# Attention in turns of two slots, with the second sigmoid written to SBUF

## The chip, the cores and the metric

The kernel runs on one core of a Trainium2 chip. A core has TensorE (PE) for matmuls, VectorE (DVE), ScalarE (ACT) and GpSimd (POOL) for elementwise work, and SyncE (SP), from whose queue most transfers are issued. The metric is the device time of one execution in microseconds (us). Before the change it was 1052.52 us, the median of three runs (1050.96 to 1053.29).

## The reference

Three stages follow each other: a sigmoid attention, a mixture of experts with one expert per token, and a feed-forward layer. The change is in the attention alone:

```python
def _attn_ref(q, k, v):                      # each (4, 12, 448, 64)
    S = q.shape[2]
    scale = 1.0 / np.sqrt(q.shape[-1])
    scores = scale * np.matmul(q, k.transpose(0, 1, 3, 2)) - np.log(S)
    attn = 1.0 / (1.0 + np.exp(-scores))
    return np.matmul(attn, v).astype(np.float32)
...
    x = attn_out.transpose(0, 2, 1, 3).reshape(B * S, H * D)   # 1792 tokens x 768
    x = _moe_ref(x=x, **moe_kwargs)          # 8 experts, argmax routing, relu, gate weight
    return _moe2_ref(x=x, **moe2_kwargs)     # (h - tanh(h)) @ w_out
```

## The kernel before, in words

All matmul operands are split into a high part (rounded to the matmul's format) and a low part (the rest), and each product is three matmuls: high by high, low by high, high by low.

The 12 heads of the 4 batches are 24 pairs of two heads. `load` brings the raw keys and queries of a pair into a buffer `kq` (three of them, in turn) and its values into `vr`; all go out from SP's queue. `prep` makes the high part `w..h` from `kq` on DVE (L199) and the low part `w..l` on POOL (L202, two operations); `prep_v` makes `vh` on DVE (L210) and `vl` on POOL (L211), two operations each.

The scores are computed transposed, 128 keys by 448 queries. Two heads of a pair have three full tiles of 128 keys each and a rest of 64 keys; two pairs together are seven **slots**: three of the first pair, one shared slot with both pairs' rests, three of the second pair. Each slot holds two tiles of 128 x 448. In six of the seven slots the two tiles of a step are two matmuls over 64 rows of the array, which run side by side; in the shared slot they are matmuls over all 128 rows, one after the other. There are 84 slots.

For a slot `u`, `scores(u)` issues the score matmuls into `pq` in PSUM (L233; three buffers of two banks in the pool `ps2`, which `pr` of `rows` and `prank` of the routing also use). ACT then computes the sigmoid twice from `pq`: once rounded, into `ah` in SBUF (L240), and once in full, back into `pq` in PSUM (L241). DVE subtracts the two into `al` (L242). Three slots later (`LAG` = 3) `av` sums attention by values: six matmuls over 128 rows into `pav` (L256). When the last slot of a pair is summed, `pav` is copied to `xT`; `rows` transposes it on PE into `pr` (L281), which DVE copies out as `u` and `rec`. When a batch's last pair is through, its tokens are routed: `square` on ACT (L298), and `route_a`, `gate` and `route_b` with many small DVE operations.

The order on PE in the attention is the written one (`manual_schedule`): for each slot the scores, then the sums of three slots before, then what `plan` put at that slot (`prep`, `load`, `rows`, routing). The other engines' order is set by a scheduler from the program's order and its own estimates. A buffer comes free when its last reader is done.

Of the kernel before, what the change touches and what calls it, by code (L numbers as in the profile page):

```python
# [10 lines left out]
F32 = mybir.dt.float32  # L11
F32R = mybir.dt.float32r
BF16 = mybir.dt.bfloat16
I32 = mybir.dt.int32
U32 = mybir.dt.uint32
AF = mybir.ActivationFunctionType
ALU = mybir.AluOpType
# [4 lines left out]
LAG = 3  # L22
# [3 lines left out]
CONV = 14  # L26
# [3 lines left out]
P = 128  # L30
CP = 112
# [3 lines left out]
def f32(ap):  # L35
    return ap.bitcast(F32)


class Prog:
# [90 lines left out]
    def attention(self):  # L130
# [4 lines left out]
        nc, tc = self.nc, self.tc  # L135
# [10 lines left out]
        pav2 = self.pool("aps3", 2, cx, space=PSUM)  # L146

        self.ep = pers
        NV, NW, NK = 2, 2, 3
        KW = 4 * P  # L150
        kqs, ws, vhs, vls = [], [], [], []

# [19 lines left out]
        def load(i):  # L172

            b, j = pairs[i]
            kq = kqs[i % NK]
            k, q = self.k[b, j], self.q[b, j]
            for dst, src in (
                (kq[:D, KW:], q[:, :S]),
                (kq[D:, KW:], q[:, S:]),
                (kq[:D, :S], k[:, :S]),  # L180
                (kq[D:, : 3 * P], k[:, S + HK :]),
                (kq[D:, S:KW], k[:, S : S + HK]),
            ):
                nc.sync.dma_start(dst, src)
            vr = raw.tile([P, 2, 4, D], F32, tag="vr", name="vr")
            self.w_dma = nc.sync.dma_start(vr.rearrange("p h c d -> p (h c d)"), self.v[b, j])
            st[i] = dict(kq=kq, vr=vr)

        def prep(i):

            s = st[i]
            kq, (h, l) = s["kq"], ws[i % NW]
            s["w"] = (h, l)
            ks, qs = slice(0, KW), slice(KW, KW + S)
            if i == 0:
                nc.vector.tensor_copy(h[:, qs], kq[:, qs])
                nc.scalar.copy(h[:, ks], kq[:, ks])
            else:
                nc.vector.tensor_copy(h, kq)  # L199
            for x in (qs, ks):  # L200
                eng = nc.vector if i == 0 else nc.gpsimd
                eng.tensor_tensor(l[:, x], kq[:, x], f32(h[:, x]), ALU.subtract)  # L202
# [21 lines left out]
        def scores(u):  # L224
            hi = sp.tile([P, 2, S], F32R, tag="ah", name="ah", bufs=LAG + 2)
            lo = sp.tile([P, 2, S], F32R, tag="al", name="al", bufs=LAG + 2)
            tiles[u] = (hi, lo)
            pq = ps2.tile([P, 2, 512], F32, tag="qk", name="pq")
            for m, (kt, qt) in enumerate(((0, 0), (0, 1), (1, 0))):
                for x, (i, a, c, _) in enumerate(slots[u]):  # L230
                    w = st[i]["w"]
                    p = slice(0, P) if a == 2 else slice(a * D, (a + 1) * D)
                    nc.tensor.matmul(  # L233
                        pq[:, x, :S], w[kt][p, c : c + P], w[qt][p, KW:], start=(m == 0), stop=(m == 2)
                    )
            k = len(slots[u])
            pv = pq[:, :k, :S]
            sc = dict(bias=self.bias_s, scale=1.0 / math.sqrt(D))
            hi, lo = hi[:, :k], lo[:, :k]
            nc.scalar.activation(hi, pv, AF.Sigmoid, **sc)  # L240
            self.last_sig = nc.scalar.activation(pv, pv, AF.Sigmoid, **sc)  # L241
            nc.vector.tensor_tensor(lo, pv, f32(hi), ALU.subtract)  # L242

        def av(u):
            hi, lo = tiles.pop(u)
            for x, (i, a, c, o) in enumerate(slots[u]):
                s = st[i]
                vh, vl = s["v"]
                if "pav" not in s:
                    s["pav"], s["units"] = pav2.tile([P, 512], F32, tag="av", name="pav"), 0  # L250
                pav = s["pav"]
                vo = lambda t: t[:, o : o + 2].rearrange("p h d -> p (h d)")
                b0, e = s["units"] == 0, s["units"] == 6
                s["units"] += 1
                for m, (vv, aa) in enumerate(((vh, hi), (vl, hi), (vh, lo))):
                    nc.tensor.matmul(  # L256
                        pav[:, :S], vo(vv), aa[:, x], start=(b0 and m == 0), stop=(e and m == 2)
                    )
                if e:
                    b, j = pairs[i]  # L260
                    if j == 0:
                        self.bts[b] = dict(
                            rec=self.recs[b % 2],
                            ss=self.sm.tile([CP, NCH], F32, tag="ss", name="ss"),
                            u=xp.tile([CP, NCH, E], F32, tag="u", name="u"),
                        )
                    s["xT"] = xp.tile([P, S], F32, tag="xT", name="xT")
                    if i % 2:
                        nc.scalar.copy(s["xT"], pav[:, :S])
                    else:  # L270
                        nc.vector.tensor_copy(s["xT"], pav[:, :S])  # L271
# [22 lines left out]
                nc.gpsimd.tensor_copy(rec[:, :, self.DM : self.DM + 1], self.tok[:, b].unsqueeze(2))  # L294

        def square(bt, c):
            sq = xp.tile([CP, NJ * P], F32, tag="sq", name="sq", bufs=1)
            nc.scalar.activation(sq, bt["rec"][:, c, : NJ * P], AF.Square, accum_out=bt["ss"][:, c : c + 1])  # L298

        self.cv, self.n_early = None, NEARLY  # L300
# [1 line left out]
        def conv():  # L302

            while self.units and self.n_early:
                if self.cv is None:
                    self.cv = self.conv_steps(*self.units[0], after=self.w_dma)
                    self.units.pop(0)
                with tc.high_priority(offset=LATER):
                    r = next(self.cv, 1)
                if r is None:  # L310
                    return
                self.cv = None
                self.n_early -= 1
# [13 lines left out]
            warm = self.cp.tile([P, 1], F32, name="warm")  # L327
            nc.scalar.activation(warm, self.bias_s, AF.Sigmoid)
        prep(0)
        for i in (1, 2):  # L330
            if i < n:
                load(i)
        if n > 1:
            prep(1)
        prep_v(0)
        pe = {mybir.EngineType.PE}
        with tc.manual_schedule(engines=pe):
            at = {}

            def plan(u, f, *args):  # L340
                at.setdefault(u, []).append((f, args))

            def events(u):
                while at.get(u):
                    f, args = at[u].pop(0)
                    f(*args)
                at.pop(u, None)

            def route(i):
                b = pairs[i][0]  # L350
                bt = self.bts.pop(b)
                for c in range(NCH):
                    plan(now[0] + 1 + c // 2 if b < B - 1 else now[0], square, bt, c)
                r = self.route_a(bt)
                pr = lambda: ps1.tile([P, 2, 512], F32, tag="qk", name="prank")
                if b == B - 2:
                    plan(now[0] + ROUTE_E - 1, self.gate, b, r)
                    plan(now[0] + ROUTE_E, self.route_b, b, r, pr)
                    plan(now[0] + ROUTE_E, self.send_rows, b, r)
                    plan(now[0] + ROUTE_E, self.early_rows)  # L360
                    plan(ns, self.early_gates)
                    plan(ns + 1, self.early_columns, lambda: ps2.tile([P, 2, 512], F32, tag="qk", name="xt"))
                elif b < B - 1:
                    plan(now[0] + ROUTE - 1, self.gate, b, r)
                    plan(now[0] + ROUTE, self.route_b, b, r, pr)
                    plan(now[0] + ROUTE, self.send_rows, b, r)
                else:
                    self.last_route = b, r

            for i in range(n):  # L370
                if i >= 2:
                    plan(final[i - 2] + 1, prep, i)
                if i >= 3:
                    plan(final[i - 3] + 2, load, i)
                if i >= 1:
                    plan(first[i] + LAG - 2, prep_v, i)
                plan(final[i] + LAG + ROW + (3 if i == 0 else 0), rows, i)
                if pairs[i][1] == NJ - 1:
                    plan(final[i] + LAG + ROW, route, i)
            plan(5, self.embedding)  # L380
            now = [0]
            u = 0
            while u < ns + LAG:
                now[0] = u
                if u < ns:
                    scores(u)
                if LAG <= u < ns + LAG:
                    av(u - LAG)
                events(u)
                if u >= CONV:  # L390
                    conv()
                if u == ns and self.cv is not None:
                    for _ in self.cv:
                        pass
                u += 1
        while at:
            now[0] = u
            events(u)
# [772 lines left out]
```

## Time and profile before

| what | value |
|---|---|
| median of three runs | 1052.52 us |
| the profiled execution | 1052.65 us |
| its span | 1050.9 us |
| PE, DVE, ACT, POOL busy | 97%, 79%, 53%, 16% of the span |
| mean granted TensorE clock | 0.995 |
| the last `pr` of the attention starts on PE at | 238.08 us |

The profile gives, for one execution, the busy time of each engine, and the trace lists every instruction with its start, its duration and, where the engine was idle before it, what released it. Matmuls are pipelined, so that a PE row lasts longer than the step to the next row; the steps between starts tell the pace.

### The profile page before, as it was taken

To read this page: it belongs to the slowest core of one execution; us is meant where nothing else is said; L and a number is where in the kernel's file an instruction comes from. 1 tells how busy PE (TensorE), PEld (TensorE's weight loads), DVE (VectorE), ACT (ScalarE), POOL (GpSimd) and SP (SyncE) were. 2 spreads that over 40 slices of the span, in tenths; PEclk is the share of its full clock that TensorE was granted. 3 is DMA by queue.
4 is the path that set the end of the run, shared out by engine and by line. 5 is a ranking of instruction groups with operands and counts; after the bars stand their busy time and mean duration, and the time that the engine had idled before them with its cause. 6 is when DMAs were issued, how large, how long until landed. Compare 5 with 4: busy or idle time off the path is not lost.

```text
span 1050.9 us, 16813 instructions
## 1 busy us (share of the span) xinstructions
PE 1016.5 (97%) x6437; PEld 939.6 (89%) x6437; DVE 828.9 (79%) x1172; ACT 557.0 (53%) x694; POOL 166.4 (16%) x178
## 2 busy tenths in 40 slices
PE   7999999899999999999998999999999999999997
PEld 5777777678999999999997899999999999999997
DVE  7879797978968878889963798888987676766774
ACT  6778787777666666666643544442453322332230
POOL 7345546342021001010000000000000300000002
PEclk9999999999999999999999999999999999999999
DMA  5422424338878984874922535454443522332212
GB/s 160 140 83 82 134 65 142 118 115 299 297 243 299 337 290 162 282 257 161 309 103 94 197 139 175 180 210 150 181 151 120 193 94 89 120 120 98 113 61 106
DMA packets 83527, 175.28 MB, mean 167 GB/s; under 512 B 7639, under 2 KB 62958, under 8 KB 83438
## 3 DMA queue, kind: packets, MB, share of 16 engines
q1 hardware_dynamic: 79598, 155.78, 43.2%
q0 software_dynamic: 3840, 18.35, 4.9%
q8 instruction: 52, 0.85, 0.3%
q14 instruction: 37, 0.30, 0.1%
HBM read 156.68 MB, written 36.30 MB: 184 GB/s over the span
## 4 chain that ended last, share of the span: by engine, by line
issue 57%; PE 29%; DVE 8%; POOL 3%; DMA 2%; ACT 1%; SPq 0%; POOLq 0%; DVEq 0%; ACTq 0%
PE pty L786 8%; PE pth L786 8%; PE pav L256 6%; PE pq L233 4%; POOL out_dram L491 2%; DVE al L242 2%; PE pr L281 1%; DVE vh L210 1%; DMA xg<-x_tok,gidx 1%; DVE wl L777 1%; PE xt L725 1%; DMA cr<-in_moe_w_in_dram 1%; ACT wh L776 1%; POOL vl L211 0%; DVE xT L271 0%
## 5 line engine op out<-in xcount | busy, mean ns | idle before, releaser
L1041 PE MATMUL o<-wo,gh 128*128 128x384 f32 x896 | 240.8, 335 | 0.7 <-DVE acc L1054 0.7
L1001 PE MATMUL z<-yh,wi 128*128 128x448 f32 x768 | 221.2, 370 | 4.1 <-ACT yh L973 3.8
L1041 PEld LDWEIGHTS o<-wo,gh 128*128 128x128 f32 x896 | 163.3, 188 | 2.3 <-DVE acc L1054 1.0
L1001 PEld LDWEIGHTS z<-yh,wi 128*128 128x128 f32 x768 | 144.3, 189 | 16.9 <-ACT yh L973 4.2
L1041 PE MATMUL o<-wo,gl 128*128 128x384 f32 x448 | 150.1, 335 | 0.1
L1001 PE MATMUL z<-yl,wi 128*128 128x448 f32 x384 | 138.0, 367 | 0.0
L786 PE MATMUL pth<-wi,wh 128*128 128x256 f32 x432 | 121.4, 282 | 2.9 <-ACT wi L729 1.2
L1054 DVE TENSOR_TENSOR acc<-o,acc 128x768 f32<-128x768 f32 x97 | 92.4, 952 | 39.5 <-PE o L1041 38.3
L786 PE MATMUL pty<-hh,wl 128*128 128x256 f32 x432 | 121.7, 284 | 0.2 <-DVE wl L777 0.2
L786 PE MATMUL pth<-wi,wl 128*128 128x256 f32 x432 | 121.3, 281 | 0.3 <-DVE wl L777 0.3
L786 PE MATMUL pty<-hh,wh 128*128 128x256 f32 x432 | 121.5, 285 | 0.0
L786 PE MATMUL pty<-hl,wh 128*128 128x256 f32 x432 | 121.3, 283 | 0.0
L786 PE MATMUL pth<-xl,wh 128*128 128x256 f32 x432 | 120.9, 280 | 0.0
L240 ACT ACTIVATE ah<-pq,bias_s 128x896 fp32r<-128x896 f32 x84 | 85.2, 1014 | 45.5 <-PE pq L233 45.5
L242 DVE TENSOR_TENSOR al<-pq,ah 128x896 fp32r<-128x896 f32 x84 | 90.4, 1084 | 23.8 <-ACT pq L241 23.3
L491 POOL DMA_INDIRECT out_dram<-acc,toki x14 | 17.2, 1232 | 577.9 <-DVE acc L1054 576.7
L1024 ACT CAST gh<-r 128x896 fp32r<-128x896 f32 x32 | 30.0, 938 | 135.1 <-DVE r L1022 82.2
L1008 ACT ACTIVATE t<-z 128x896 f32<-128x896 f32 x32 | 29.4, 920 | 127.3 <-PE z L1001 73.8
L777 DVE TENSOR_TENSOR wl<-w1raw,wh 128x768 fp32r<-128x768 f32 x72 | 68.2, 955 | 25.0 <-ACT wh L776 24.3
L1041 PEld LDWEIGHTS o<-wo,gl 128*128 128x128 f32 x448 | 84.1, 188 | 1.7 <-DVE gl L1025 0.4
L786 PEld LDWEIGHTS pth<-wi,wh 128*128 128x128 f32 x432 | 81.6, 189 | 3.5 <-ACT wi L729 1.4
L786 PEld LDWEIGHTS pty<-hh,wl 128*128 128x128 f32 x432 | 82.4, 191 | 0.4 <-DVE wl L777 0.4
(249 smaller groups left out, 2200.4 us busy)
## 6 DMA issues: line engine op xcount, KB each, us to landing
w1raw<-in_moe_w_dram SPq DMA_DIRECT2D x36, 768.0 KB
w2raw<-in_moe_w_dram SPq DMA_DIRECT2D x27, 1024.0 KB
wi<-dwi SPq DMA_DIRECT2D x32, 768.0 KB
wo<-dwo SPq DMA_DIRECT2D x32, 768.0 KB
cr<-in_moe_w_in_dram SPq DMA_DIRECT2D x16, 768.0 KB
dwi<-cr SPq DMA_DIRECT2D x16, 768.0 KB
cr<-in_moe_w_out_dram SPq DMA_DIRECT2D x16, 768.0 KB
dwo<-cr SPq DMA_DIRECT2D x16, 768.0 KB
```

What stands on the lines that cost most here:

```text
L233: nc.tensor.matmul(pq[:, x, :S], w[kt][p, c : c + P], w[qt][p, KW:], start=(m == 0), stop=(m == 2))
L240: nc.scalar.activation(hi, pv, AF.Sigmoid, **sc)
L242: nc.vector.tensor_tensor(lo, pv, f32(hi), ALU.subtract)
L256: nc.tensor.matmul(pav[:, :S], vo(vv), aa[:, x], start=(b0 and m == 0), stop=(e and m == 2))
L491: i = self.nc.gpsimd.indirect_dma_start(**kw)
L777: nc.vector.tensor_tensor(wl, cols, f32(wh), ALU.subtract)
L786: nc.tensor.matmul(pt[:, u], a[:, kk], b[:, kk], start=(n == 0), stop=(n == 3 * K - 1))
L1001: nc.tensor.matmul(z[:, g, :GT], wi[:, a, j * P : (j + 1) * P], b[:, j], start=(n == 0), stop=(n == 3 * NJ - 1),)
L1008: nc.scalar.activation(t, zv, AF.Square)
L1024: nc.scalar.copy(gv, r)
L1041: nc.tensor.matmul(o[:, w, :NW], a[:, u, i * P : (i + 1) * P], wo[:, b, w * NW : (w + 1) * NW], start=(n == 0), stop=(n == 3 * CH - 1),)
L1054: nc.vector.tensor_tensor(acc[i], ov, acc[i], ALU.add)
```

## The change

Three things change. The loop over slots takes two slots per turn: the scores of both, then the sums of both slots that are due, then the planned events of both. The second sigmoid goes to a new SBUF tile `af` (two buffers), and `al` is `af` less `ah`. To make room the raw keys and queries have two buffers instead of three, so that the third pair's load follows the second pair's `prep`, and `sq`, whose contents nobody reads, is BF16.

```diff
--- before.py
+++ after.py
@@ -146,7 +146,7 @@
         pav2 = self.pool("aps3", 2, cx, space=PSUM)
 
         self.ep = pers
-        NV, NW, NK = 2, 2, 3
+        NV, NW, NK = 2, 2, 2
         KW = 4 * P
         kqs, ws, vhs, vls = [], [], [], []
 
@@ -238,8 +238,9 @@
             sc = dict(bias=self.bias_s, scale=1.0 / math.sqrt(D))
             hi, lo = hi[:, :k], lo[:, :k]
             nc.scalar.activation(hi, pv, AF.Sigmoid, **sc)
-            self.last_sig = nc.scalar.activation(pv, pv, AF.Sigmoid, **sc)
-            nc.vector.tensor_tensor(lo, pv, f32(hi), ALU.subtract)
+            af = sp.tile([P, 2, S], F32, tag="af", name="af", bufs=2)[:, :k]
+            self.last_sig = nc.scalar.activation(af, pv, AF.Sigmoid, **sc)
+            nc.vector.tensor_tensor(lo, af, f32(hi), ALU.subtract)
 
         def av(u):
             hi, lo = tiles.pop(u)
@@ -294,7 +295,7 @@
                 nc.gpsimd.tensor_copy(rec[:, :, self.DM : self.DM + 1], self.tok[:, b].unsqueeze(2))
 
         def square(bt, c):
-            sq = xp.tile([CP, NJ * P], F32, tag="sq", name="sq", bufs=1)
+            sq = xp.tile([CP, NJ * P], BF16, tag="sq", name="sq", bufs=1)
             nc.scalar.activation(sq, bt["rec"][:, c, : NJ * P], AF.Square, accum_out=bt["ss"][:, c : c + 1])
 
         self.cv, self.n_early = None, NEARLY
@@ -327,11 +328,9 @@
             warm = self.cp.tile([P, 1], F32, name="warm")
             nc.scalar.activation(warm, self.bias_s, AF.Sigmoid)
         prep(0)
-        for i in (1, 2):
-            if i < n:
-                load(i)
-        if n > 1:
-            prep(1)
+        load(1)
+        prep(1)
+        load(2)
         prep_v(0)
         pe = {mybir.EngineType.PE}
         with tc.manual_schedule(engines=pe):
@@ -381,18 +380,22 @@
             now = [0]
             u = 0
             while u < ns + LAG:
-                now[0] = u
-                if u < ns:
-                    scores(u)
-                if LAG <= u < ns + LAG:
-                    av(u - LAG)
-                events(u)
-                if u >= CONV:
-                    conv()
-                if u == ns and self.cv is not None:
-                    for _ in self.cv:
-                        pass
-                u += 1
+                two = range(u, u + 2)
+                for v in two:
+                    if v < ns:
+                        scores(v)
+                for v in two:
+                    if LAG <= v < ns + LAG:
+                        av(v - LAG)
+                for v in two:
+                    now[0] = v
+                    events(v)
+                    if v >= CONV:
+                        conv()
+                    if v == ns and self.cv is not None:
+                        for _ in self.cv:
+                            pass
+                u += 2
         while at:
             now[0] = u
             events(u)
```

On PE, in the first stretch of full turns (first pairs; `pq` are scores, `pav` the sums), before:

```order
L233 MATMUL pq<-w0h 128x448 x2
L233 MATMUL pq<-w0l,w0h 128x448 x2
L233 MATMUL pq<-w0h,w0l 128x448 x2
L256 MATMUL pav<-ah,vh_206 128x448
L256 MATMUL pav<-ah,vl_207 128x448
L256 MATMUL pav<-al,vh_206 128x448
L256 MATMUL pav<-ah,vh_206 128x448
L256 MATMUL pav<-ah,vl_207 128x448
L256 MATMUL pav<-al,vh_206 128x448
L233 MATMUL pq<-w0h 128x448 x2
L233 MATMUL pq<-w0l,w0h 128x448 x2
L233 MATMUL pq<-w0h,w0l 128x448 x2
```

And now, from the same score matmuls on:

```order
L233 MATMUL pq<-w0h 128x448 x2
L233 MATMUL pq<-w0l,w0h 128x448 x2
L233 MATMUL pq<-w0h,w0l 128x448 x2
L233 MATMUL pq<-w0h 128x448 x2
L233 MATMUL pq<-w0l,w0h 128x448 x2
L233 MATMUL pq<-w0h,w0l 128x448 x2
L257 MATMUL pav<-ah,vh_203 128x448
L257 MATMUL pav<-ah,vl_204 128x448
L257 MATMUL pav<-al,vh_203 128x448
L257 MATMUL pav<-ah,vh_203 128x448
L257 MATMUL pav<-ah,vl_204 128x448
L257 MATMUL pav<-al,vh_203 128x448
```

The scores of the next slot have moved ahead of the sums, and six more sums follow those shown here, before the next scores.

On DVE, one period of seven slots in the first batch (`al` the difference of the sigmoids, `vh` and `w..h` the casts, `xT`, `u` and `rec` copies out of PSUM), before:

```order
L199 CAST w1h<-kq_191 128x960
L271 COPY xT<-pav 128x448
L210 CAST vh_202<-vr 128x4x64 x2
L242 TENSOR_TENSOR al<-pq,ah 128x896 x3
L291 TENSOR_TENSOR u<-pr,u 112x32
L292 COPY rec_193<-pr 112x4x128
L210 CAST vh_206<-vr 128x4x64 x2
L242 TENSOR_TENSOR al<-pq,ah 128x896
L199 CAST w0h<-kq_192 128x960
L242 TENSOR_TENSOR al<-pq,ah 128x896 x2
L291 TENSOR_TENSOR u<-pr,u 112x32
L292 COPY rec_193<-pr 112x4x128
```

And now:

```order
L199 CAST w1h<-kq_191 128x960
L272 COPY xT<-pav 128x448
L210 CAST vh_199<-vr 128x4x64 x2
L243 TENSOR_TENSOR al<-af,ah 128x896 x3
L210 CAST vh_203<-vr 128x4x64 x2
L243 TENSOR_TENSOR al<-af,ah 128x896
L292 TENSOR_TENSOR u<-pr,u 112x32
L293 COPY rec_192<-pr 112x4x128
L199 CAST w0h<-kq_190 128x960
L243 TENSOR_TENSOR al<-af,ah 128x896 x2
L292 TENSOR_TENSOR u<-pr,u 112x32
L293 COPY rec_192<-pr 112x4x128
```

The second two `vh` and one `al` have moved ahead of `u` and `rec`; `al` reads `af` where it read `pq`, and the casts of `w` take turns between two `kq` instead of three.

## Rows read from the trace of the kernel before

**Rows 1.** The page: busy time, share of the span and instructions of each engine.
```profile
PE 1016.5 (97%) x6437; PEld 939.6 (89%) x6437; DVE 828.9 (79%) x1172; ACT 557.0 (53%) x694; POOL 166.4 (16%) x178
```
**Rows 2.** Busy us (x instructions) by stretch: start:end, length, PE, PEld, DVE, ACT, POOL, clock, DMA.
```profile
77.00:104.00 27.00, 25.34 (x148) 18.98 (x147) 25.65 (x51) 23.18 (x32) 12.72 (x14) 1.00 0.25 72
104.00:132.00 28.00, 27.94 (x160) 21.73 (x159) 21.45 (x32) 20.59 (x23) 16.08 (x17) 1.00 0.48 137
...
187.00:218.00 31.00, 26.44 (x153) 19.67 (x151) 30.66 (x116) 23.74 (x33) 12.62 (x13) 1.00 0.28 88
```
**Rows 3.** Waits of PE, first 260 us: waiter, releaser, total us, times, longest.
```profile
PE pq L233 <- DVE al L242: 5.4, 5, 1.5
```
**Rows 4.** Timeline of PE: start us, duration us, engine, line, operation, tiles, shapes, count.
```profile
178.09 0.37 PE L233 MATMUL pq<-w0h,w0l 64*128 64x448 f32 x2
178.38 0.48 PE L256 MATMUL pav<-ah,vh 128*128 128x448 f32 x1
178.70 0.37 PE L256 MATMUL pav<-ah,vl 128*128 128x448 f32 x1
178.91 0.36 PE L256 MATMUL pav<-al,vh 128*128 128x448 f32 x1
...
179.51 0.37 PE L256 MATMUL pav<-al,vh 128*128 128x448 f32 x1
179.72 0.36 PE L233 MATMUL pq<-w0h 128*128 128x448 f32 x1
```
**Rows 5.** Groups by line: tiles, shapes, count, busy us, mean ns, idle before, releaser.
```profile
L242 DVE TENSOR_TENSOR al<-pq,ah 128x896 fp32r<-128x896 f32 x84 | 90.4, 1084 | 23.8 <-ACT pq L241 23.3
L240 ACT ACTIVATE ah<-pq,bias_s 128x896 fp32r<-128x896 f32 x84 | 85.2, 1014 | 45.5 <-PE pq L233 45.5
...
L241 ACT ACTIVATE pq<-pq,bias_s 128x896 f32<-128x896 f32 x84 | 82.2, 979 | 0.0
...
L1025 DVE TENSOR_TENSOR gl<-r,gh 128x896 fp32r<-128x896 f32 x32 | 34.8, 1088 | 9.8 <-ACT gh L1024 9.6
```
**Rows 6.** Timelines of POOL and DVE, 88 to 104 us.
```profile
90.08 2.40 POOL L202 TENSOR_TENSOR w0l<-kq,w0h 128x448 fp32r<-128x448 f32 x2 [0.72 <-POOL vl L211]
...
90.94 0.31 DVE L125 SCALAR_TENSOR_TENSOR t<-t,nr 112x4 f32<-112x4 f32 x1
91.28 1.21 DVE L126 TENSOR_TENSOR t<-t,ss 112x4 f32<-112x4 f32 x1
```
**Rows 7.** Timelines of DVE and POOL, 36 to 56 us.
```profile
42.94 0.95 DVE L899 TENSOR_TENSOR cr<-ca,cr 128x768 fp32r<-128x768 f32 x1
...
43.11 3.09 POOL L202 TENSOR_TENSOR w1l<-kq,w1h 128x448 fp32r<-128x448 f32 x2 [7.78 <-DVE w1h L199]
```
**Rows 8.** Timeline of DVE, one period of seven slots.
```profile
113.33 0.68 DVE L292 COPY yT_last<-pr 112x512 f32<-112x512 f32 x1
115.39 1.09 DVE L242 TENSOR_TENSOR al<-pq,ah 128x896 fp32r<-128x896 f32 x1 [1.38 <-ACT pq L241]
...
119.64 2.07 DVE L242 TENSOR_TENSOR al<-pq,ah 128x896 fp32r<-128x896 f32 x2
...
127.86 1.09 DVE L242 TENSOR_TENSOR al<-pq,ah 128x896 fp32r<-128x896 f32 x1 [0.92 <-ACT pq L241]
129.89 1.09 DVE L242 TENSOR_TENSOR al<-pq,ah 128x896 fp32r<-128x896 f32 x1 [0.94 <-ACT pq L241]
...
131.00 0.68 DVE L292 COPY yT_last<-pr 112x512 f32<-112x512 f32 x1
```
**Rows 9.** Timeline of POOL, the same period.
```profile
117.12 2.45 POOL L202 TENSOR_TENSOR w1l<-kq,w1h 128x448 fp32r<-128x448 f32 x2 [2.38 <-DVE w1h L199]
119.53 1.49 POOL L211 TENSOR_TENSOR vl<-vr,vh 128x256 fp32r<-128x256 f32 x2
124.49 0.73 POOL L211 TENSOR_TENSOR vl<-vr,vh 128x256 fp32r<-128x256 f32 x1 [3.48 <-DVE vh L210]
...
127.02 2.39 POOL L202 TENSOR_TENSOR w0l<-kq,w0h 128x448 fp32r<-128x448 f32 x2 [0.83 <-DVE w0h L199]
```

## The prediction

> **What bounds the kernel now.** I read the page first, then a table by stretch, then the timelines of PE, DVE and POOL side by side. PE is busy 97% of the span [rows 1], which names no single wait; the change touches only the attention, about the first 238 us, so that part is cut into stretches. Two kinds alternate there. In 104 to 132 us PE is busy 27.94 of 28 us and DVE 21.45: PE sets the pace. In 187 to 218 us DVE is busy 30.66 of 31 us and PE only 26.44: there a batch is routed and DVE sets the pace; 77 to 104 us is the same more weakly [rows 2]. Where PE waits for DVE it is mostly for a scores buffer that `al` has not yet been read out of, 5.4 us in five waits [rows 3].
>
> **What a turn costs on PE.** Matmuls of 448 columns start 0.20 to 0.21 us apart. At a change between the score matmuls, which use 64 rows of the array, and the sums, which use 128, both the last step before it and the first behind it take 0.29 to 0.32 us: 178.09 to 178.38 and 178.38 to 178.70, against 178.70 to 178.91. The shared slot's scores use 128 rows, and from 179.51 to 179.72 there is no gap [rows 4]. So a change costs 0.2 us. Six of seven slots are of the 64-row kind, 72 of the 84, and each now has a change in and a change out: 144. Two slots per turn leave two changes per turn, with or without a shared slot in it, 42 x 2 = 84. The first part of the change removes 60 x 0.2 = 12.0 us of PE time. A period of seven slots takes 17.7 us where PE sets the pace (113.33 to 131.00) [rows 8], 12 changes among it; with 7 on the mean it needs 16.7 us.
>
> **What the second sigmoid in SBUF costs on ACT.** ACT's sigmoid into SBUF takes 1014 ns and into PSUM 979 [rows 5]: 84 x 35 ns = 2.9 us more ACT work. ACT is busy 20.59 of 28 us in the PE-paced stretch [rows 2], so PE's pace hides it; were that cover gone, 2.9 us would be its price.
>
> **What it costs on DVE by itself.** `al` from PSUM and SBUF takes 1084 ns, and the later `gl`, the same shape with both inputs in SBUF, 1088 ns [rows 5]: no difference. The Trainium skill ("Perfetto Trace Analysis", Optimizing Scalar/DVE Operations) gives DVE about 60 ns of access overhead on SBUF against 125 on PSUM, which would make 84 `al` 5.5 us cheaper; the two rows do not show it, and the sum takes nothing.
>
> **What it costs by meeting POOL.** This is the term that decides. POOL subtracts `wl` and `vl` from SBUF tiles all through the attention. A DVE operation with two SBUF inputs does not run beside that: L126 on 4 elements per partition starts at 91.28 and takes 1.21 us, to the end of POOL's second `w0l` at 92.48, and L125 ends with POOL's first one [rows 6]. The other way round, POOL's pair of subtractions beside L899 (two SBUF inputs, from 42.94) takes 3.09 us [rows 7], against 2.39 and 2.45 elsewhere [rows 9]. `al` from PSUM runs freely today: two of them take 2.07 us from 119.64 [rows 8] while POOL does both `vl` from 119.53 [rows 9]. Afterwards `al` reads `af` and `ah`, both SBUF, so it and POOL's operations take turns.
>
> The Trainium skill states this as a rule ("SBUF — State Buffer", Who interferes with whom): a DVE instruction with two SBUF inputs contends with a GpSimd instruction that reads SBUF, and the one that starts second fully blocks. The trace agrees, by the 1.21 us above. Without the rule the sum would be that of the PE term alone, in the lower bound below.
>
> *PE-paced periods.* In the period from `rec` at 113.33 to `rec` at 131.00 DVE idles 4.2 us (six waits, the first 1.38 and the last 0.94) [rows 8], and POOL works 2.45 + 1.49 + two times 0.74 + 2.39 = 7.8 us [rows 9]. DVE's own work, start to start in those rows, is 7 `al` x 1.0, two casts of `w` x 0.57, four of `vh` x 0.2, one `xT` of 0.54 and two times `u` and `rec` x 0.7 = 10.9 us. `xT`, `u` and `rec` read PSUM and can run beside POOL, 1.9 us. So DVE and POOL in turns need 10.9 + 7.8 = 18.7 us when nothing overlaps and 16.8 when all 1.9 does. `xT` always meets `wl`; of the two `u` and `rec`, by the new order on DVE, one meets `vl` and one finds POOL idle: 18.7 - 0.54 - 0.7 = 17.5 us. I take that, above PE's 16.7 and 0.2 below today's 17.7. (Walking through today's rows with turns gives 18.0: the two `al` of 119.64 wait for one `vl` each, a cast of `w` 0.7, and the `al` of 127.86 and 129.89 wait 1.0 and 1.3 for `w0l`: 4.5 on 13.5.) The PE-paced stretches (10 to 77, 104 to 132, 160 to 187, 218 to 236) are 140 us or 7.9 periods: 7.9 x -0.2 = -1.6 us.
>
> *DVE-paced stretches.* In 88 to 104, 143 to 160 and 187 to 218 DVE has no idle to give, and each meeting of `al` with POOL that is free today lengthens them. Going through both timelines: an `al` beside `w0l` 0.9 and one beside `vl` 0.7 in each of the first two, and 0.7 + 0.7 + 1.1 + 0.7 in the third: 6.4 us. The ramps before the first two (11 us each, DVE idle 0.7) add 1.3 each, 2.6. Against it stands what the earlier release of the scores buffers gives. Today a slot on PE takes 9 x 0.203 + 2 x 0.2 = 2.2 us, and the scores behind a `pr` (0.9) need the buffer of two slots before: due after 2 x 2.2 + 0.9 = 5.4 us, with scores, two sigmoids and `al` done after 0.8 + 2.0 + 1.1 = 3.9, so 1.5 us to spare. Afterwards the scores wait for ACT, and the first to wait for `al` are the sums of the next turn, due 4.1 + 1.4 + 1.2 = 6.7 us after the turn begins, with `al` done at 0.6 + 2.0 + 1.1 = 3.7: 3.0 us to spare. That is 1.5 us gained once per stretch, 4.5. Net +4.5 us.
>
> **Edits that cost nothing.** Two buffers of keys instead of three: a load now follows POOL's `wl` of two pairs before, and the cast comes two pairs later, so of 16.7 us some 13.6 are left after 0.7 + 2.4 of cast and subtraction, where three buffers leave some 22. On SP's queue the loads of later pairs, `vr` and the early expert weights stand behind it; the weights are not used before 238 us. `sq` in BF16 changes the output of 16 ACT operations that nobody reads. The memsets of the third buffer (two) go, before PE starts. Behind the new wait of `af` for its buffer (two of them) stand ACT's next sigmoids; DVE gets the next `al` one ACT operation, 0.9 us, after the previous one ends, and needs 1.0 for the one between.
>
> **Sum.** The profiled run took 1052.65 us (span 1050.9 and 1.75 around it), the median of three 1052.52. After the attention the work on PE follows in the same form, so the shift reaches the end whole: 1052.65 - 1.6 + 4.5 = 1055.6 us. Bounds: if `al` met nothing, the periods give 7.9 x -1.0 and the stretches -4.5: -12.4, 1040. If nothing overlaps, 7.9 x +1.0 and +9.0 without the credit: +17, 1070.
>
> **Rivals.**
> *POOL fits into DVE's idle and PE stays the bound (faster).* POOL's operations can slip into the copies from PSUM and into DVE's waits for ACT, then a period costs 16.8 us, 7.9 x -0.9 = -7.1, and the routed stretches come out even: 1045.5 us. For it: 1.9 us of copies and 4.2 us of idle per period. Against it: idle is what disappears as PE speeds up. It decides where a period falls below about 17.2 us.
> *The two cancel.* At 17.2 us a period gains 0.5, 7.9 x -0.5 = -4.0, against +4.5: 1053 us, no change.
> *Keys come late (slower).* If POOL falls behind by more than the 13.6 us, the cast of `w` waits at the head of DVE and everything behind it does; 1 us at each of 21 pairs gives 1074 us. Against it: POOL has 7.8 us of work in a period and was never that late.
>
> **How the numbers follow.** Forecast (DVE and POOL in turns cost more than the changes of array rows give back) 0.50, own range 1054 to 1067; faster rival 0.33; cancelling 0.14; late keys 0.03. About 0.2% (2.1 us) is what a measurement can tell from no change. So faster 0.33, same 0.14, slower 0.53. The range 1044 to 1067 takes in the faster rival and most of the upper bound.
>
> **What would show it.** Right: POOL's pair of `wl` or DVE's `al` last clearly longer than 2.4 and 1.08 us where they meet; DVE's waits for ACT shrink from 5.4 us in a PE-paced stretch; PE's steps at a turn are 0.3 us only twice per two slots. Wrong: `al` stays at 1.08 us beside POOL, or the period of seven slots comes out at 16.7 us, or the routed stretches get shorter, or DVE waits for keys.

## The result: slower by 0.75%

The changed kernel takes 1059.69 us (median of four runs, 1058.83 to 1062.62), the kernel before 1052.43 in the runs beside it: a ratio of the means of 1.0075, with a 95% interval of 1.0062 to 1.0087. The forecast was 1055.6 with a range of 1044 to 1067 and slower as the likeliest side. The profiled execution has a span of 1058.7 us, 7.8 more than before.

The page of the changed kernel, busy time of each engine, answers to [rows 1]:

```profile
PE 1011.4 (96%) x6437; PEld 946.8 (89%) x6437; DVE 851.2 (80%) x1170; ACT 557.7 (53%) x694; POOL 210.9 (20%) x178
```

PE is busy 5.1 us less, DVE 22.3 more and POOL 44.5 more, though neither DVE nor POOL got anything more to do: the time is spent standing. `al` alone makes up 22.0 us of DVE's (112.4 against 90.4 [rows 5]). The table by stretch of the changed kernel (start:end, length, busy PE, PEld, DVE, ACT, POOL, granted clock, DMA) answers to [rows 2]:

```profile
77.00:104.00 27.00, 23.52 (x144) 19.25 (x143) 26.24 (x50) 22.86 (x32) 15.47 (x12) 1.00 0.29 80
104.00:132.00 28.00, 25.41 (x141) 20.29 (x140) 25.29 (x26) 18.40 (x22) 21.59 (x18) 0.94 0.39 123
...
187.00:218.00 31.00, 27.18 (x158) 21.87 (x157) 30.48 (x109) 23.72 (x32) 14.87 (x13) 0.94 0.38 116
```

In 104 to 132 us PE was the bound before, with 27.94 of 28 us. Now it is busy 25.41, and DVE has gone from 21.45 to 25.29; the granted clock of the stretch has fallen from 1.00 to 0.94. The array itself does what was forecast. At a turn two steps of PE take 0.30 us, the one before the change and the one behind it, and the others 0.20:

```profile
112.17 0.37 PE L233 MATMUL pq<-w1h,w1l 64*128 64x448 f32 x2
112.47 0.47 PE L257 MATMUL pav<-ah,vh 128*128 128x448 f32 x1
112.77 0.36 PE L257 MATMUL pav<-ah,vl 128*128 128x448 f32 x1
112.97 0.36 PE L257 MATMUL pav<-al,vh 128*128 128x448 f32 x1
```

The groups by line show who stands (busy us, mean ns of one, idle before and its releaser); the first two answer to [rows 5]:

```profile
L243 DVE TENSOR_TENSOR al<-af,ah 128x896 fp32r<-128x896 f32 x84 | 112.4, 1354 | 8.1 <-ACT af L242 7.9
L242 ACT ACTIVATE af<-pq,bias_s 128x896 f32<-128x896 f32 x84 | 84.9, 1011 | 9.9 <-DVE al L243 9.6
...
L211 POOL TENSOR_TENSOR vl<-vr,vh 128x256 fp32r<-128x256 f32 x48 | 61.3, 1294 | 13.0 <-DVE vh L210 8.4 <-issue 2.5 <-DVE t L123 1.2
...
L202 POOL TENSOR_TENSOR w0l<-kq,w0h 128x448 fp32r<-128x448 f32 x11 | 18.1, 1641 | 10.0 <-DVE w0h L199 9.9
```

The same groups of POOL, and DVE's cast `vh`, in the kernel before:

```profile
L211 POOL TENSOR_TENSOR vl<-vr,vh 128x256 fp32r<-128x256 f32 x48 | 36.1, 767 | 19.7 <-DVE vh L210 15.4 <-issue 3.7 <-POOL yT_last L294 0.3
L202 POOL TENSOR_TENSOR w0l<-kq,w0h 128x448 fp32r<-128x448 f32 x11 | 12.6, 1144 | 9.2 <-DVE w0h L199 3.9 <-issue 3.2 <-POOL vl L211 2.1
L210 DVE CAST vh<-vr 128x256 fp32r<-128x256 f32 x48 | 35.2, 754 | 4.0 <-PE pav L256 2.3 <-issue 1.1
```

`al` went from 1084 to 1354 ns on the mean, POOL's `vl` from 767 to 1294, its `w0l` of 448 columns from 1144 to 1641. DVE's idle time before `al` fell from 23.8 us [rows 5] to 8.1, so it could take in a part of this but not all. The Trainium skill ("SBUF — State Buffer", Who interferes with whom) says that a DVE instruction with two SBUF inputs contends with a GpSimd instruction that reads SBUF; these means agree with it.

What one meeting can cost is seen at 113 to 126 us. DVE first, then POOL (start us, us, engine, line, operation, tiles, shapes, count):

```profile
115.12 0.61 DVE L272 COPY xT<-pav 128x448 f32<-128x448 f32 x1
115.66 5.80 DVE L210 CAST vh<-vr 128x256 fp32r<-128x256 f32 x2
...
121.38 4.47 DVE L243 TENSOR_TENSOR al<-af,ah 128x896 fp32r<-128x896 f32 x3
```

```profile
114.13 2.37 POOL L211 TENSOR_TENSOR vl<-vr,vh 128x256 fp32r<-128x256 f32 x2
116.47 2.35 POOL L202 TENSOR_TENSOR w0l<-kq,w0h 128x448 fp32r<-128x448 f32 x2
118.78 0.18 POOL L295 COPY rec<-tok 112x4 f32<-112x4 f32 x1
118.93 2.36 POOL L202 TENSOR_TENSOR w1l<-kq,w1h 128x448 fp32r<-128x448 f32 x2
```

Two casts of 256 columns that need some 0.5 us take 5.80, the second alone 5.60 (from 115.86): it ends when POOL has gone through two `w0l` and two `w1l` that lie back to back. Then three `al`, 3.1 us of work, take 4.47 beside POOL's next `vl`. POOL had fallen behind: its issues of the token scatter `x_tok` end at 114.1 us, where before they ended at 108.8, and its work came in one piece behind them. DVE stood for the whole piece.

That is the exception. At 62 us two such casts meet two `w1l` that also lie back to back, and take 2.22 us, one POOL operation for each cast:

```profile
62.44 2.22 DVE L210 CAST vh<-vr 128x256 fp32r<-128x256 f32 x2
```

```profile
62.06 2.45 POOL L202 TENSOR_TENSOR w1l<-kq,w1h 128x448 fp32r<-128x448 f32 x2 [0.75 <-DVE w1h L199]
```

Most meetings in this trace last no longer than the rest of one POOL operation. One other wait is clearly longer, a cast of 3.16 us at 202.80, to the end of two `w0l`. Why these two are not let in between is open.

The end of the attention, PE of the changed kernel and behind it the same of the kernel before (in brackets the idle time and what ended it):

```profile
234.75 1.09 PE L282 MATMUL pr<-ien,xT 128*112 128x136 f32 x8
237.04 0.33 PE L728 MATMUL xt<-ident,xg 128*128 128x128 f32 x1 [1.20 <-ACT xg L709]
239.37 2.61 PE L728 MATMUL xt<-ident,xg 128*128 128x128 f32 x11 [2.00 <-ACT xg L709]
...
242.06 0.72 PE L257 MATMUL pav<-ah,vh 128*128 128x448 f32 x1
242.58 0.57 PE L257 MATMUL pav<-ah,vl 128*128 128x448 f32 x1
242.95 0.57 PE L257 MATMUL pav<-al,vh 128*128 128x448 f32 x1
...
247.78 0.36 PE L789 MATMUL pth<-wi,wh 128*128 128x256 f32 x1 [1.33 <-DVE yT_last L293]
```

```profile
232.88 1.09 PE L281 MATMUL pr<-ien,xT 128*112 128x136 f32 x8
233.81 1.76 PE L725 MATMUL xt<-ident,xg 128*128 128x128 f32 x12
...
236.23 0.36 PE L256 MATMUL pav<-ah,vl 128*128 128x448 f32 x1
236.43 0.37 PE L256 MATMUL pav<-al,vh 128*128 128x448 f32 x1
...
239.01 0.37 PE L786 MATMUL pth<-wi,wh 128*128 128x256 f32 x1
```

PE reaches the loop's last `pr` 1.9 us later than before, but the first expert matmul `pth` 8.8 us later. In between it waits 1.20 and 2.00 us for the early expert's gathered tokens `xg`, then does the last sums in steps of 0.37 us where before they went in steps of 0.20, and waits another 1.33 us for `yT_last`. The granted clock was 1.00 there before; in the changed kernel, after these waits, it was:

```profile
238.00:242.00 4.00, 2.63 (x13) 2.43 (x14) 0.91 (x2) 2.11 (x3) 0.00 (x0) 0.52 0.43 157
```

about half, the lower of its two levels (1.2 and 2.4 GHz). What the tokens wait for is DVE: they are scattered behind `rec`, the last step of routing that batch (a reciprocal, DVE L487 before and L490 after):

```profile
222.58 0.18 DVE L490 RECIPROCAL rec<-gs 112x4 f32<-112x4 f32 x1
```

```profile
218.07 0.17 DVE L487 RECIPROCAL rec<-gs 112x4 f32<-112x4 f32 x1
```

In the ten runs of the table below in which PE waits for `xg` at the first `xt`, this `xt` comes 14.2 to 15.6 us behind `rec`, whether `rec` is early or late.

### The profile page after: what moved, and what is told of

It reads as the page before. It is cut to its first block, busy times and chain, and to the rows that moved or that the text cites. A ratio compares the mean times of both kernels' runs of the same rounds, so it can differ in the third digit from the quotient of the medians.

```text
span 1058.7 us, 16741 instructions
## 1 busy us (share of the span) xinstructions
PE 1011.4 (96%) x6437; PEld 946.8 (89%) x6437; DVE 851.2 (80%) x1170; ACT 557.7 (53%) x694; POOL 210.9 (20%) x178
## 4 chain that ended last, share of the span: by engine, by line
issue 55%; PE 19%; DVE 6%; POOL 2%; DMA 2%; ACT 1%; POOLq 0%; SPq 0%; DVEq 0%; ACTq 0%
PE pth L789 8%; PE pty L789 8%; DVE al L243 2%; POOL out_dram L494 2%; DMA xg<-x_tok,gidx 1%; DVE vh L210 1%; PE xt L728 1%; DVE wl L780 1%; PE pav L257 1%; PE pq L233 1%; DMA x_tok<-rec,idx 0%; POOL x_tok L494 0%; DMA kq<-in_q_dram 0%; ACT wh L779 0%; DVE yT L637 0%
## 5 line engine op out<-in xcount | busy, mean ns | idle before, releaser
L243 DVE TENSOR_TENSOR al<-af,ah 128x896 fp32r<-128x896 f32 x84 | 112.4, 1354 | 8.1 <-ACT af L242 7.9
L240 ACT ACTIVATE ah<-pq,bias_s 128x896 fp32r<-128x896 f32 x84 | 84.9, 1011 | 35.6 <-PE pq L233 35.1
L242 ACT ACTIVATE af<-pq,bias_s 128x896 f32<-128x896 f32 x84 | 84.9, 1011 | 9.9 <-DVE al L243 9.6
```

Source lines behind the costliest of these rows:

```text
L242: self.last_sig = nc.scalar.activation(af, pv, AF.Sigmoid, **sc)
L243: nc.vector.tensor_tensor(lo, af, f32(hi), ALU.subtract)
```

## Experiments

Twelve runs. The first eight take the change apart. Subtractions on DVE instead of POOL take the meetings away; they also take away what PE waits for POOL's results (1.8 us for `vl` and 0.8 for `w0l` in 77 to 236 us of the changed kernel). The runs called "sigmoid to SBUF" have the changed kernel's two key buffers and BF16 `sq` as well. Medians, with the ratio to the kernel before on the same chip and its 95% interval, and three marks from one profile of each: `rec` on DVE, the first `xt` and the first expert matmul `pth` on PE.

```
                                    us     ratio (95%)             rec     xt      pth
before                           1052.4                          218.07  233.81  239.01
after                            1059.69  1.0075 (1.0062-1.0087) 222.58  237.04  247.78
turns alone                      1058.15  1.0054 (1.0036-1.0072) 222.66  238.83  244.04
sigmoid to SBUF, no turns        1060.31  1.0070 (1.0053-1.0086) 225.55  241.14  252.47
two key buffers alone            1051.38  0.9995 (0.9985-1.0006) 215.79  231.44  236.66
after, POOL's work on DVE        1045.66  0.9942 (0.9924-0.9961) 212.06  226.58  235.60
before, POOL's work on DVE       1047.29  0.9955 (0.9937-0.9972) 213.82  228.13  236.82
turns alone, on DVE              1050.49  0.9987 (0.9972-1.0002) 214.99  229.16  239.15
sigmoid to SBUF alone, on DVE    1046.63  0.9938 (0.9916-0.9959) 212.58  226.81  235.67
after, columns later             1062.18  1.0096 (1.0068-1.0124) 222.89  237.65  248.49
after, last 6 pairs on DVE       1065.34  1.0119 (1.0100-1.0138) 226.10  240.81  250.60
after, first 18 pairs on DVE     1045.20  0.9929 (0.9912-0.9945) 213.47  228.03  236.41
on DVE, columns later            1045.43  0.9936 (0.9919-0.9953) 212.63  227.53  233.78
on DVE, row copies on ACT        1044.22  0.9926 (0.9907-0.9946) 209.36  224.66  233.43
```

One profile differs from the next by some 2 us in these marks: the kernel with only the key buffers changed takes the same time as before and has `rec` 2.3 us earlier. The profile of the sigmoid to SBUF without the turns is of its longest run, 1064.66 us, so its marks are late.

**The turns alone.** The loop of the changed kernel in the kernel before; second sigmoid in PSUM, three key buffers.

```diff
-                if u < ns:
-                    scores(u)
-                if LAG <= u < ns + LAG:
-                    av(u - LAG)
+                for v in two:
+                    if v < ns:
+                        scores(v)
+                for v in two:
+                    if LAG <= v < ns + LAG:
+                        av(v - LAG)
```

> The kernel before with the turns of two slots alone: the second sigmoid stays in PSUM, three buffers of keys. Meeting theory (al with two SBUF inputs and POOL's subtractions take turns): al stays at 1.08 us, PE saves up to 12 us of changes, less some waits because pq is now held until al by both slots of a turn; the first pth on PE comes before 239 us and the time is about 1046 us (1042 to 1051). Rival (the turns themselves make PE wait): as slow as the changed kernel, 1056 to 1061 us.

Slower, 1058.15: in the rival's range, and the meeting theory missed. Its waits of PE (waiter, releaser, total us, times, longest), to be read beside [rows 3]:

```profile
PE pq L233 <- DVE al L242: 11.0, 12, 1.9
```

5.6 us more of waits for a score buffer than before: two slots ask for their buffers at once, and with the second sigmoid in PSUM a buffer comes back only after `al`. That the result is 5.7 us does not make these waits the whole of it, since PE also has up to 12 us of changes less. The granted clock fell too: 0.72 in 90 to 96 us, 0.86 in 102 to 114, 0.73 in 144 to 150 and 0.75 in 216 to 222, where the kernel before had 1.00, in all up to 6.5 us of PE's time if it had work throughout (an estimate, the share that is missing in each stretch times its length). How the loss divides was not tested. The prediction saw the earlier release of these buffers as a credit of the full change (1.5 us per stretch); that the turns without it lose more than they save it did not see.

**The sigmoid to SBUF without the turns**, with the changed kernel's other edits.

```diff
-            self.last_sig = nc.scalar.activation(pv, pv, AF.Sigmoid, **sc)
-            nc.vector.tensor_tensor(lo, pv, f32(hi), ALU.subtract)
+            self.last_sig = nc.scalar.activation(af, pv, AF.Sigmoid, **sc)
+            nc.vector.tensor_tensor(lo, af, f32(hi), ALU.subtract)
```

> The changed kernel with one slot per turn: af in SBUF, two buffers of keys, sq in BF16, the order of before. Meeting theory: the price of the meetings without the gain in changes, al near 1.35 us on the mean, 1058 to 1068 us. Rival (turns): as the kernel before, 1051 to 1054 us.

As expected by the meetings: 1060.31, with this group in its profile:

```profile
L243 DVE TENSOR_TENSOR al<-af,ah 128x896 fp32r<-128x896 f32 x84 | 111.5, 1340 | 10.9 <-ACT af L242 10.1 <-issue 0.2
```

**Two key buffers alone.** `NV, NW, NK = 2, 2, 2` and the order of the first loads, nothing else.

> The kernel before with two buffers of keys and queries alone. Both theories: no change, 1051 to 1054 us, and DVE's cast waits for no load beyond the 1.3 us of the start. Late keys (the third rival of the prediction): 1056 us or more, with DVE waiting for keys.

No change; the rival of late keys falls.

**POOL's subtractions on DVE**, in the changed kernel; the next three runs put the same edit into the kernel before, into the turns alone and into the sigmoid alone.

```diff
-                eng = nc.vector if i == 0 else nc.gpsimd
+                eng = nc.vector
-                nc.gpsimd.tensor_tensor(vl[:, o], vr[:, a], f32(vh[:, o]), ALU.subtract)
+                nc.vector.tensor_tensor(vl[:, o], vr[:, a], f32(vh[:, o]), ALU.subtract)
```

> The changed kernel with POOL's subtractions (wl and vl) on DVE, so that nothing of POOL reads SBUF beside al except the small pow operations. DVE gets 1.07 + 4 x 0.3 us or less per pair more. Meeting theory: al back at 1.08 us, a period of seven slots needs 10.9 + 2 x 1.7 = 14.3 us of DVE, below PE's 16.7; the routed stretches stay full; 1044 to 1054 us, below the changed kernel's 1059.7 in any case. Rival (turns): not below 1057 us.

1045.66, 14 us below the changed kernel and faster than both. Groups on DVE in this run:

```profile
L243 DVE TENSOR_TENSOR al<-af,ah 128x896 fp32r<-128x896 f32 x84 | 91.0, 1085 | 6.4 <-ACT af L242 6.2
...
L211 DVE TENSOR_TENSOR vl<-vr,vh 128x256 fp32r<-128x256 f32 x48 | 18.9, 416 | 0.1
...
L210 DVE CAST vh<-vr 128x256 fp32r<-128x256 f32 x48 | 12.6, 289 | 0.0
```

`al` from two SBUF tiles takes 1085 ns when POOL is quiet, so its 1354 were the meetings, as were 754 to 762 of the cast `vh`, before and after the change. The subtractions that POOL did cost DVE 416 ns a piece for `vl` and 653 for `wl`. PE now waits for something else:

```profile
PE xt L728 <- ACT xg L709: 11.4, 2, 9.7
```

> The kernel before (one slot per turn, second sigmoid in PSUM, three key buffers) with POOL's subtractions of the low halves of weights and values moved to DVE: no two engines subtract in SBUF at once. DVE then carries, by the durations of the run of after with the same move, 46 subtractions of 654 ns and 46 of 416 ns more and 46 copies of 289 instead of some 546 ns: about 0.37 us a slot more. Theory A (the gain of 13 us in that run needs the freed score banks and the two-slot turns; the meetings alone are not it): DVE reaches PE's period of 17.5 us per seven slots, no gain, 1052 to 1060. Theory B (POOL beside DVE is the whole cost, in before too): as fast as that run, 1044 to 1048.

1047.29, in the range of theory B. So 5.1 of the 14.0 us were to be had without the change under study. The four medians belong together: with POOL at work the change costs 7.3 us (1052.43 to 1059.69), with POOL quiet it gives 1.6 (1047.29 to 1045.66), which is within the scatter. The difference, 8.9 us, is what the meetings cost that the change adds. DVE has more to do, and yet its routing is done 4.3 us earlier than in the kernel before. A group of it:

```profile
L210 DVE CAST vh<-vr 128x256 fp32r<-128x256 f32 x48 | 12.6, 286 | 1.1 <-PE pav L256 0.9
```

> Turns of two slots with the second sigmoid in PSUM, subtractions on DVE. Theory A (the turns are slow because the score bank is given back only by DVE's al, and two slots ask for it at once: PE waited 11.0 us for al in the run of the turns alone): DVE has more to do, so these waits stay or grow, 1054 to 1064. Theory B (the turns alone were slow through meetings with POOL): the meetings are gone, the 12 us that PE saves show, 1040 to 1047.

1050.49, between the two theories: the turns cost 3.2 us more than no turns (1047.29) when nothing meets, 5.7 when POOL meets DVE. PE's waits for the buffer that `al` holds were 5.5 us in five without the turns and are with them:

```profile
PE pq L233 <- DVE al L242: 7.3, 11, 1.7
```

> Second sigmoid to SBUF, two key buffers, one slot per turn, subtractions on DVE. al at 1.08 us as nothing meets it. Theory A (both parts are needed: the freed banks let PE run ahead, the turns take 144 changes of the array's form down to 84, 12 us): PE is back at its period of 17.4 to 17.5 us, 1050 to 1056. Theory B (the turns give nothing, only the meetings cost): the time of the run with turns, 1045 to 1047.

1046.63, theory B again: as fast as with the turns. The turns do save PE work: up to 215 us it is busy 199.94 us for 1192 matmuls with them and 206.90 for 1173 without. But `rec` comes at 212.58 without them and 212.06 with them, and what is left of PE's saving at the end of the loop is a longer wait for the tokens, 9.7 us where without the turns the longest is 6.2:

```profile
PE xt L724 <- ACT xg L705: 7.8, 2, 6.2
```

**Columns later.** In the changed kernel, `early_columns` planned one turn later, so that PE does the last sums before the transposes `xt`.

```diff
-                    plan(ns + 1, self.early_columns, lambda: ...
+                    plan(ns + 2, self.early_columns, lambda: ...
```

> The changed kernel with the early expert columns' attention sums and projection planned one turn earlier on PE, ahead of the transposes of the gathered tokens instead of behind them (nothing else moves). Theory A (of the 7.8 us that the first expert matmul comes later than before, some 6 arise in the tail: PE waits 1.20 and 2.00 us for the gathered tokens with this work still queued behind, and does it afterwards at half the clock, 242.06 to 246.5): the first expert matmul at 243 to 245 instead of 247.8, the time 1055 to 1057.5. Rival (the chain from the routing to the gather to the transposes to the expert sets the end whatever PE does beside it, and the loss is in the loop): 1058.5 to 1061.

1062.18, slower than the changed kernel and above both ranges, and the edit did not do what it says alone. ACT's timeline in this run:

```profile
239.69 3.03 ACT L779 CAST wh<-w1raw 128x768 fp32r<-128x768 f32 x4
242.62 1.56 ACT L732 CAST wi<-xt 128x512 fp32r<-128x512 f32 x3
```

Only PE's order is written by hand; on ACT and DVE the planner put the weights' casts `wh` ahead of `wi`, the cast that the first expert matmul needs. It settles nothing on the tail.

**Where in the attention.** The subtractions on DVE for the last six of 24 pairs only (`i >= 18`), and for the first 18 only (`i < 18`).

```diff
-                eng = nc.vector if i == 0 else nc.gpsimd
+                eng = nc.vector if i == 0 or i >= 18 else nc.gpsimd
```

> The changed kernel with POOL's subtractions of the last six of 24 pairs (from about 169 us) on DVE; those of the first 18 stay on POOL. With all of them on DVE the changed kernel is 14 us faster (1045.7 against 1059.7); this run and the next ask where in the attention these 14 us arise. Theory A (meetings cost everywhere, but only DVE's lateness in the last stretch, where the early expert's tokens are routed, reaches the end whole): the last stretch falls from 53 to 51 us and the routing comes 3 to 5 us earlier, 1053 to 1057. Rival (lateness of any stretch is carried to the end, the stretch before 169 us holds 18 of 24 pairs and so most of it): 1056.5 to 1060.

> The changed kernel with POOL's subtractions of the first 18 pairs on DVE; the last six pairs stay on POOL. Theory A (the end feels most of all the last stretch): 1052 to 1056. Rival (lateness of any stretch is carried on): al number 60 comes as early as in the run with all on DVE (158 instead of 178 us), the last six pairs then lose some 3 us, 1047 to 1050.

The first misses both ranges (1065.34, slower than the changed kernel), the second is below them (1045.20). Start of `al` number 78 (from 0), by DVE's timelines: 223.2 in the changed kernel, 218.7 with the late pairs on DVE, 214.1 with the early ones, 204.7 with all. So DVE's lateness is carried on from every stretch, and the late pairs give 4.5 us there. But the first expert does not wait for `al`, it waits for `rec`:

```profile
226.10 0.18 DVE L490 RECIPROCAL rec<-gs 112x4 f32<-112x4 f32 x1
```

In DVE's instruction order `rec` stands behind 78 of the 84 `al` in the kernels before and after and with the early pairs on DVE, and behind 82 with the late pairs on DVE. The planner, which sets DVE's order from its own costs, let four more `al` pass, and PE, done with its work, waited:

```profile
240.81 0.48 PE L728 MATMUL xt<-ident,xg 128*128 128x128 f32 x1 [9.89 <-ACT xg L709]
```

With all of them on DVE it is 82 too: there `rec` comes 7.4 us behind `al` number 78. A version in which DVE gains these 18.5 us at `al` number 78 (223.2 to 204.7) and `rec` keeps its old place was not tried, so that the order is what made the late pairs slow is read from the timelines, not shown by a run.

**Two candidates on top of it.** With all subtractions on DVE, the columns later (as above), and in another kernel the copies of the projected rows of the first 20 pairs on ACT:

```diff
-            nc.vector.tensor_copy(xr.rearrange("p (a c) d -> p a c d", a=2), pv[:, :, :, :P])
+            (nc.scalar.copy if i < 20 else nc.vector.tensor_copy)(xr.rearrange("p (a c) d -> p a c d", a=2), pv[:, :, :, :P])
```

> A candidate: the changed kernel with all subtractions on DVE, and the early expert's transposes planned one turn later on PE, so that the last sums and the last projection of the attention run while PE waits for the gathered tokens (9.69 us at 226.58 in the run with the subtractions on DVE). ACT's order moves with it: its four wh casts now stand ahead of xg, in the same idle time, where in the earlier run with this edit they stood between the transposes and their casts wi (which made it slower, 1062.2). Theory A (the gather's chain sets when the tokens come, and all that stood behind it moves ahead of it): first expert matmul at 231 to 233 instead of 235.6, 1041 to 1043.5. Rival (behind the transposes something else sets the end, wl or the half clock after the idle): 1045 to 1048.

> A candidate: the changed kernel with all subtractions on DVE and the copies of the projected rows out of PSUM (512 columns, 0.68 us) of the first 20 pairs on ACT, 13.6 us less on DVE, which is busy 102.56 of 110 us from 77 to 187; ACT was busy 93.4. Theory A (DVE's pace sets when the early tokens are routed): gather and transposes come 5 to 10 us earlier, 1037 to 1042. Rival (ACT becomes the bound, 93.4 + 7 of 110 us with its sigmoids behind each copy; or the meetings were all there was): 1044 to 1049.

The first is 1045.43, in the rival's range. PE's timeline shows the work moved into the wait:

```profile
218.27 0.36 PE L257 MATMUL pav<-al,vh 128*128 128x448 f32 x1
227.53 0.48 PE L728 MATMUL xt<-ident,xg 128*128 128x128 f32 x1 [8.90 <-ACT xg L709]
...
233.78 0.36 PE L789 MATMUL pth<-wi,wh 128*128 128x256 f32 x1
```

From `rec` to `pth` it is 21.2 us instead of 23.5 and `pth` comes 1.8 us earlier, but the time is the same within its scatter; where the 2 us went is open. The second is the lowest median, 1044.22, at the lower edge of the rival's range: DVE in 77 to 187 us falls from 102.56 to 96.79 us, ACT rises from 93.42 to 99.11, `rec` comes 2.7 us earlier for 13.6 us taken off DVE, and PE waits in a new place:

```profile
PE pq L233 <- ACT af L242: 4.6, 5, 2.0
```

These two, the run on DVE and the one with the early pairs on DVE have intervals that overlap; each beats both kernels.

## Why the prediction came out as it did

- **The side and its cause were right.** `al` meeting POOL costs more than the change gives. Sending the second sigmoid to SBUF, without the turns, shows it: the time goes from 1052.43 to 1060.31 with POOL at work and from 1047.29 to 1046.63 without, so 8.5 us come from meetings. The size was too small, +2.9 us against +7.3, and the range of 1044 to 1067 took in the faster rival too, so that it holds the result says little.
- **Changes of the array's form.** Right as a price: two steps of 0.30 us at a turn, the others 0.20. Wrong as a gain: the turns are worth 0.6 us with the meetings (1060.31 against 1059.69) and 1.0 us without (1046.63 against 1045.66), both within scatter, because DVE's progress to `rec`, not PE, sets when the expert starts. The rival "POOL fits and PE stays the bound" named 1045.5, near the 1045.66 with POOL quiet; but PE is not the bound there either, it waits 11.4 us for the tokens.
- **ACT's 35 ns and `al` by itself** came out as said: 1011 against 979 ns in PSUM, and 1085 ns from SBUF.
- **The meetings.** Predicted net: -1.6 us in PE-paced stretches and +4.5 in DVE-paced ones, +2.9. Measured, after minus before, at the start of `al` number 8, 29, 36, 43, 57, 64, 71, 78: +2.2, -0.6, -0.9, +2.7, +3.2, +3.7, +1.4, +5.0 us. So the mostly PE-paced spans among these (up to 29, 36 to 43, 57 to 64) gave +2.2 - 2.8 + 3.6 + 0.5 = +3.5 and the others -0.3 + 0.5 - 2.3 + 3.6 = +1.5. The parts miss by 5.1 us one way and 3.0 the other; that their sum comes within 2.1 us, no more than profiles differ by, is luck. The mis-sized term is the period of 17.5 us, with DVE and POOL taking turns one operation at a time. The period from `al` 36 to 43 took 21.2 us (before 17.6): it holds the 5.80 us above, DVE held through POOL's whole backlog. The one from 71 to 78, in the last routed stretch, took 23.7 (before 20.1) and holds the cast of 3.16 us. Others were shorter than forecast (16.5 from 15 to 22).
- **"The shift reaches the end whole"** is the step that failed. PE's loop ends +1.9 us (forecast +2.9), within the scatter of profiles, but the first expert matmul comes 8.8 us later. DVE is 4.5 us late with `rec`, and from `rec` to `pth` it takes 25.2 us instead of 20.9. PE, which saves its changes in the last stretch, runs dry and waits 3.2 us for the tokens, does what is left at half the clock, and waits 1.33 us for `yT_last`. Over all runs this part is 20.9 to 21.4 us where PE comes to `xt` without a wait for `xg` (before, turns alone, two key buffers) and 22.9 to 26.9 where it waits, but for the run that moved work into the wait (21.2). The late columns were meant to show it and did not, and on top of the subtractions on DVE they brought `pth` forward without bringing the time down; so the share of clock and wait in the 4.3 us is argued from the two timelines, not shown by a run.
- **Edits at nothing.** Two key buffers: shown in the kernel before, ratio 0.9995. The squares in BF16 were not run alone.

## What to carry to other kernels

Before giving an engine a second SBUF input to free a PSUM bank, look who else reads SBUF then. Most meetings here cost the rest of one instruction of the other engine, but a few cost its whole backlog, so look where its work piles up. Moving POOL's subtractions onto DVE, some 48 us there, made this kernel faster although DVE was the busiest engine but PE: look at durations that differ for the same shape. And find the instruction that releases the next phase (here one reciprocal on DVE) and follow its place in the order; an edit, even one elsewhere, can move it.

## What the runs showed of the hardware that I had not expected

- A cast with one SBUF input suffers as a two-input subtraction does: `vh`, 256 columns, 754 ns on the mean with POOL at work and 286 without. The prediction counted only the waits of two-input operations as new and took the cast at 0.2 us.
- A DVE operation can stand through several POOL operations that lie back to back: 5.60 us for one cast, four subtractions and a copy long. The Trainium skill ("SBUF — State Buffer", Summary: rules for kernel authors) says that of two that contend the second to issue blocks until the first finishes. Most meetings of this trace agree with it, as the 2.22 us for two casts at 62 us; the 5.60 us do not, and no run here shows why.
